# The first token group's product with w3 from split fp16 operands, with a new preparation and order of the weights

## The chip, the cores and the metric

The kernel runs on one core of one Trainium2 chip. The metric is the time of one execution on the device in microseconds (us); below, "the time" is the median of the runs shown. TensorE is PE in the profile, its weight loads are PEld, VectorE is DVE, ScalarE is ACT, GpSimd is POOL, and SP is the engine that issues most of the DMAs.

## The reference

Two layers, each of a local dilated attention (block A) and an MLP mixer (block B), are applied twice to 2048 tokens of 512 features. Everything is float32. Cut to what matters:

```
x = A_x
for layer in (0, 1):
    x = x + A(layernorm(x), wqkv, wo)        # 32 heads of 16; each token sees 8 tokens, 2 apart
    x = x + B(layernorm(x), w1, w2, w3, w4)

def B(x, w1, w2, w3, w4):                    # w3: 512 x 1792, w4: 1792 x 512
    h  = gelu(layernorm(x) @ w1)
    hs = (quarters of h shifted by +1, -1, +2, -2 tokens) @ w2
    x1 = x + hs
    return x1 + gelu(layernorm(x1) @ w3) @ w4
```

## The kernel before, in words

**Tiles and groups.** The 2048 tokens are 4 blocks of 512, and each block is 4 tiles of 128 tokens. With two layers there are 8 steps n = 0 to 7, one per layer and block. In step n the functions are: `p1_quarters`/`p1_stream` (layer norm and the product with wqkv; the results go to DRAM and come back with the neighbours' rows), `p2_unit` (the attention itself, almost all on VectorE: a product `prod<-kv,q`, a reduction into `L`, a softmax, a product `prod<-kv,L`, additions), `p3` (the product with wo, then norm and w1), `p4` (shift, the product with w2, norm), `p5` (w3, gelu, w4). Because w2 needs shifted rows, `p4` and `p5` work on a *group* of tiles that lags by one tile: group 0 has 3 tiles (384 tokens), later groups have 4, the last has 5.

**Split operands.** Most products replace one float32 product by three fp16 products. Each operand is written as hi + lo, two fp16 numbers, and `HLS` (line 50) names the three pairs hi·hi, hi·lo and lo·hi that are summed in PSUM. The weights wqkv, wo, w1, w2 are split on the chip near the start and kept. w3 and w4 are 14 chunks each; they are split by `big_pair` (line 912) and stored in DRAM as `w34_d`. A pair is two chunks of w3 and two of w4: four loads, four squares on ScalarE with a sum (tile `ss_p`), a product with ones and a power that give the scale (`power_of`, line 541), and for each chunk `hi_of` (583), `rest` (590) and a DMA that stores it. `p5` loads them again for each group (`w<-w` in the profile).

**Group 0 is the exception** (`PLAIN = 1`, line 1242). Its normalized tiles are turned by TensorE in float32 (`turn_f32`, line 698) and copied by ScalarE into `nT`. For each chunk, `plain_chunk` (line 1297) loads w3 and w4 once more in float32 straight from the input, forms the w3 product in float32 (four matmuls 128x128 by 128x384, which the profile records as eight), applies gelu, and forms the w4 product in float32 (three matmuls of 512 columns, recorded as six). Later groups turn their tiles by DMA (`turn_dma`, line 675): ScalarE writes the hi half, VectorE or GpSimd the lo half, and SP issues one DMA transpose.

**What sets the order.** Every operation gets a number in the order in which the code creates it. The list `PLACES` (line 56) gives each its place in one global order, written out by hand. `plan` (line 268) walks that order, gives out buffers, and issues each operation on its engine; `InOrder` (line 328) keeps each engine's instructions in that order (all instructions carry line 338 in the profile for this reason). `OTHER` (line 196) lists the operations that take their second alternative, mostly GpSimd in place of VectorE or ScalarE. The durations in the code feed only `plan`'s choice of buffers. Each engine, and SP's queue of DMAs, is therefore a fixed sequence: an instruction that waits holds up all that stand behind it on its engine.

**Buffers that matter here.** `w` (8), `g` (5), `nT` (2), `mm` (4 PSUM banks), `prod` (1) and `kv` (3).

Of the kernel before, what the change touches and what calls it, by code (L numbers as in the profile page):

```python
# [56 lines left out]
15 29 72 33 3 148 0 1 6 5 19 12 8 13 7 21 40 58 20 45 2 4 14 16  # L57
17 9 10 11 24 26 18 22 23 30 31 36 37 39 48 50 28 35 25 27 44 46 42 43
49 53 47 55 54 63 51 62 71 76 201 67 61 110 64 90 73 98 74 109 177 422 132 117
92 119 111 156 112 165 130 169 396 311 275 391 104 137 168 221 202 203 236 237 360 374 252 413  # L60
96 75 204 115 41 52 32 34 56 59 38 57 60 65 77 79 80 91 94 121 86 93 82 95
81 99 85 102 87 103 84 101 83 100 131 114 136 158 159 174 175 176 195 246 285 239 313 322
323 364 384 435 524 462 523 155 186 213 218 267 289 321 575 339 588 488 499 434 437 526 558 551
574 547 578 482 538 589 591 598 603 611 618 620 623 685 694 642 645 693 668 669 670 900 922 823
845 864 912 868 924 932 939 943 952 958 965 987 978 998 1000 953 973 1021 961 972 1053 433 436 408
409 426 431 387 432 438 453 470 472 561 581 604 508 566 567 473 485 573 483 491 634 891 908 870
981 886 942 928 944 982 1008 1013 1020 1034 1035 1046 1027 1030 1044 1070 1087 1088 1085 1110 1121 786 787 781
782 799 801 780 804 808 816 821 826 860 861 862 838 839 847 834 836 925 865 866 927 1023 1048 969
994 977 1005 1007 1052 1054 1068 1076 1082 1111 1123 1144 1083 1089 1092 1086 1107 1108 1131 1148 1175 146 199 153
183 135 219 150 184 232 234 235 244 258 516 637 305 331 543 309 325 358 260 282 452 105 144 253  # L70
97 318 278 506 448 1084 78 70 69 152 68 66 107 127 133 140 141 149 160 166 167 191 192 193
205 208 220 212 216 223 229 280 290 296 128 116 120 126 171 154 198 222 145 164 151 210 211 245
250 257 277 281 283 287 300 304 335 301 308 317 348 349 394 403 170 173 182 181 310 217 243 306
224 242 249 263 279 299 314 329 350 353 359 376 380 388 397 390 400 410 411 412 416 423 273 270
297 298 332 405 371 407 357 366 361 381 392 393 398 399 402 404 415 418 420 442 444 419 441 443
451 458 465 466 106 108 122 123 124 138 147 194 196 230 185 188 190 189 178 179 200 180 88 89
125 129 143 162 163 225 227 238 226 228 233 231 240 264 268 265 241 271 291 319 320 324 328 356
368 373 363 395 445 446 369 379 417 421 157 161 207 274 276 288 292 336 370 378 326 362 377 375
333 334 337 338 450 454 622 477 512 533 560 521 520 705 577 582 593 614 616 621 641 644 662 671
687 688 695 698 701 702 703 704 707 708 753 721 722 725 727 735 736 737 744 748 749 784 592 597  # L80
752 633 658 706 713 610 571 732 666 667 678 686 731 733 734 742 743 755 759 760 761 762 763 764
765 766 771 777 805 767 768 769 770 772 773 774 775 809 810 811 113 142 187 197 209 214 215 261
272 284 247 259 266 262 269 293 295 294 172 206 248 251 254 255 256 302 303 312 307 315 342 347
316 327 346 341 286 365 383 385 386 401 427 430 484 504 428 455 486 487 464 490 517 503 118 134
139 340 343 367 372 389 414 447 382 459 481 460 406 425 480 468 696 692 849 745 747 820 822 783
803 802 829 850 856 888 889 892 899 905 906 909 910 911 915 917 929 940 948 957 1091 1149 1232 963
975 993 1003 1022 1037 1045 1058 1119 1130 1239 872 933 1161 1067 1079 1094 1095 835 966 1170 1112 1113 1127 1128
1136 1137 1141 1151 1152 1177 1179 1180 1181 1182 1183 1186 1187 1197 1199 1210 1225 1198 1207 1208 1209 1212 1214 1215
1233 1234 1237 1238 344 345 429 440 457 463 469 497 519 544 471 505 522 518 545 556 584 576 351 352
474 475 476 479 489 525 546 548 511 535 947 848 554 579 580 632 534 536 537 557 559 583 602 664  # L90
697 710 890 914 945 986 657 718 751 788 461 478 552 553 555 568 572 635 663 665 817 831 951 832
601 612 837 625 1206 1043 1263 1235 1242 1271 1277 1224 1226 1292 1248 1253 1257 1258 1278 1293 1294 1295 1303 1304
1306 1321 1322 1323 1324 1325 1327 1338 1402 1418 1421 1483 1484 1485 1486 1489 1490 1492 1493 1531 1532 1562 1320 1218
1401 1343 1344 1363 1364 1366 1367 1420 1377 1381 1403 1404 1415 1419 1430 1435 1436 1437 1439 1455 1461 1462 1468 1469
1470 1471 1480 1497 1543 1503 1521 1522 1525 1526 1527 1528 1529 1534 1545 1565 456 330 354 439 355 424 449 467
492 493 500 501 502 527 532 496 498 513 514 515 529 530 494 495 507 528 539 540 541 509 510 531
542 549 550 562 605 563 569 570 587 617 590 564 585 586 600 852 565 595 596 599 628 630 594 606
# [1337 lines left out]
```

## Time and profile before

| what | value |
|---|---|
| runs | 1142.68, 1144.0 and 1894.58 us; median 1144.0 us |
| the profiled execution's own time | 1145.03 us |
| its span, first to last instruction | 1143.2 us |
| mean granted TensorE clock | 0.997 |
| busy PE / DVE / ACT / POOL | 98% / 75% / 54% / 37% |
| DMA moved | 206.37 MB, mean 181 GB/s |

The profiled execution's time is 1.8 us longer than its span; the median of the runs is 1.03 us below that time. In a timeline row stand the start, the length, the engine, the line, the operation with out<-in, the count that was merged, and in brackets the idle time before it with what ended it. In a row of stages stand the stretch, its length, and for PE, PEld, DVE, ACT and POOL the busy time with the number of instructions, then the granted clock, the DMA engines' busy share and GB/s. A matmul's recorded length overlaps the next one's, so the cost of a run of matmuls is read from start to start.

### The profile page before, as it was taken

Reading aid. Unit: us, or ns where it says so; the run is one execution under the profiler, and the core shown is the slowest. Engines: PE = TensorE matmul, PEld = TensorE weight load, DVE = VectorE, ACT = ScalarE, POOL = GpSimd, SP = SyncE. Lnnn points to the kernel's source line nnn. Section 1 sums busy time; section 2 is a strip of 40 time slices with the busy share of each in tenths; the row PEclk is TensorE's granted clock in tenths of the full one; section 3 lists DMA queues with packets and bytes.
Section 4 is the critical chain, followed back from the end, with each engine's and each line's share of the span. In section 5 each row is a group of like instructions: output and inputs, shape, how many; then the busy total and the mean of one; then the engine's idle time right before and its main releaser. Section 6 shows DMA issues by size and latency. Waiting matters only on the chain.

```text
span 1143.2 us, 15112 instructions
## 1 busy us (share of the span) xinstructions
PE 1124.1 (98%) x5190; PEld 532.4 (47%) x5190; DVE 862.6 (75%) x919; ACT 618.6 (54%) x1089; POOL 417.9 (37%) x596
## 2 busy tenths in 40 slices
PE   8989999999999999999999999999999999999998
PEld 6544445554444444444444444444444444444554
DVE  4989899997899998988888888378986888323212
ACT  4766785247863565464654565354555554535321
POOL 4342364125652571135534353252324342322000
PEclk9999999999999999999999999999999999999999
DMA  6988989997989669974679756596687865524322
GB/s 175 217 205 215 223 216 259 256 238 182 265 234 222 162 161 211 244 187 121 161 182 230 192 136 166 128 237 177 154 206 166 199 168 158 113 75 112 100 88 79
DMA packets 249165, 206.37 MB, mean 181 GB/s; under 512 B 131032, under 2 KB 192472, under 8 KB 249088
## 3 DMA queue, kind: packets, MB, share of 16 engines
q1 hardware_dynamic: 247472, 203.63, 72.3%
q10 hardware_dynamic: 1616, 1.77, 0.5%
q8 instruction: 41, 0.67, 0.2%
q14 instruction: 36, 0.29, 0.1%
HBM read 132.64 MB, written 37.87 MB: 149 GB/s over the span
## 4 chain that ended last, share of the span: by engine, by line
PE 60%; ACT 2%; DVE 1%; issue 1%; POOL 1%; POOLq 0%; DVEq 0%; ACTq 0%
PE mm L338 42%; PE acc L338 18%; POOL small L338 1%; ACT f L338 1%; DVE L L338 0%; DVE prod L338 0%; ACT junk L338 0%; DVE f L338 0%; ACT L338 0%; ACT g L338 0%; ACT mm L338 0%; POOL f L338 0%; DVE x L338 0%; POOL o L338 0%; DVE h L338 0%
## 5 line engine op out<-in xcount | busy, mean ns | idle before, releaser
L338 PE MATMUL acc<-w,g 128*128 128x512 f16 (+1 forms) x1260 | 307.3, 394 | 0.0
L338 PE MATMUL mm<-nT,w 128*128 128x512 f16 (+1 forms) x1288 | 301.7, 389 | 0.8 <-ACT f L338 0.8
L338 PE MATMUL mm<-wq_hl,xt 128*128 128x512 f16 x1008 | 226.8, 381 | 3.2 <-DMA xt<-f 2.3
L338 ACT ACTIVATE mm<-mm,s_w 128x512 f32<-128x512 f32 (+1 forms) x144 | 89.7, 628 | 195.0 <-PE mm L338 194.7
L338 PEld LDWEIGHTS <-w 128*128 128x128 f16 x1344 | 125.2, 98 | 142.2 <-issue 1.0
L338 PEld LDWEIGHTS <-g 128*128 128x128 f16 x1176 | 114.7, 98 | 137.5
L338 DVE TENSOR_TENSOR prod<-kv,L 128x2048 f32<-128x2048 f32 x64 | 148.7, 2325 | 13.6 <-POOL o L338 12.2
L338 PEld LDWEIGHTS <-xt 128*128 128x128 f16 x1008 | 98.8, 98 | 122.5 <-issue 4.8
L338 DVE TENSOR_REDUCE L<-prod 128x128 f32<-128x2048 f32 x64 | 146.2, 2284 | 1.2
L338 POOL TENSOR_SCALAR small<-small 128x1 f32<-128x1 f32 (+1 forms) x200 | 88.8, 444 | 137.8 <-ACT junk L338 123.8
L338 DVE TENSOR_TENSOR prod<-kv,q 128x2048 f32<-128x2048 f32 x58 | 134.3, 2316 | 3.7 <-DMA q<-q_d 1.9
L338 DVE TENSOR_TENSOR prod<-prod 128x512 f32<-128x512 f32 (+2 forms) x109 | 111.5, 1026 | 2.7
L338 POOL TENSOR_TENSOR g<-f,g 128x512 f16<-128x512 f32 x39 | 54.8, 1409 | 117.8 <-ACT g L338 69.2
L338 DVE SCALAR_TENSOR_TENSOR g<-mm,c_g,g 128x512 f16<-128x512 f32 x56 | 41.5, 745 | 63.7 <-ACT g L338 63.7
L338 PE MATMUL mm<-w_hl,h 128*128 128x512 f16 x384 | 85.7, 379 | 1.1 <-POOL h L338 1.1
L338 PE MATMUL mm<-nT,w_hl 128*128 128x512 f16 x384 | 86.5, 379 | 0.0
L338 POOL TENSOR_TENSOR small<-small,nhalf 128x1 f32<-128x1 f32 (+1 forms) x104 | 72.3, 695 | 8.7
L338 PE MATMUL mm<-wo_hl,oT 128*128 128x512 f16 x336 | 74.3, 379 | 0.0
L338 POOL TENSOR_TENSOR prod<-prod 128x512 f32<-128x512 f32 (+1 forms) x24 | 30.5, 1271 | 105.9 <-DVE prod L338 99.4
L338 ACT ACTIVATE ev<-mm,s_kv 128x512 f32<-128x512 f32 x56 | 38.1, 681 | 54.8 <-PE mm L338 40.0
L338 ACT ACTIVATE g<-mm,c_g 128x512 f16<-128x512 f32 x98 | 66.6, 684 | 1.9
L338 PEld LDWEIGHTS <-oT 128*128 128x128 f16 x426 | 41.5, 98 | 49.0 <-issue 0.6
(188 smaller groups left out, 1217.8 us busy)
## 6 DMA issues: line engine op xcount, KB each, us to landing
w<-w SPq DMA_DIRECT2D x196, 256.0 KB
kv<-kv_d SPq DMA_DIRECT2D x112, 352.0 KB
w<-in_B_w_dram SPq DMA_DIRECT2D x56, 256.0 KB
kv_d<-ev SPq DMA_DIRECT2D x112, 128.0 KB
q_d<-ev SPq DMA_DIRECT2D x28, 256.0 KB
w<-g SPq DMA_DIRECT2D x28, 256.0 KB
q<-q_d SPq DMA_DIRECT2D x28, 256.0 KB
x<-x SPq DMA_DIRECT2D x26, 256.0 KB
```

What stands on the lines that cost most here:

```text
L338: i = f(*a, **k).ins
```

## The change

Group 0's w3 product takes the same three fp16 products as the others, from the split `w34_d`, at a width of 384; its w4 product stays in float32. The w3 loads in float32 of `p5(0)` (14 of 256 KB) become loads of `w34_d`. Group 0's three tiles are turned by DMA. w3 and w4 are split in groups of four chunks (4, 4, 4, 2), all of w3 ahead of all of w4, and the scale `s_w3` is made per group of w3 chunks.

```diff
-BY_DMA = {"p1": 1, "p2": 1, "p3": 1, "p4": 1}
+BY_DMA = {"p1": 1, "p2": 1, "p3": 1, "p4": 0}
...
-    def big_pair(c, key):
+    def big_four(k, j, key):
...
-    iv = [big_pair(c, KW + 0.6 + 0.2 * c) for c in range(NP)]
+    iv = [big_four(k, j, KW + 0.6 + 0.4 * k + 0.1 * j) for k in range(2) for j in range(len(FOURS))]
...
+        if k == 0:
+            def inverse():
+                v = s_w3.t[:, cs[0]:cs[0] + len(cs)]
+                V.tensor_scalar(v, iv4.t, SN, None, ALU.mult)
+                V.reciprocal(v, v)
+            dve(key, 0.3, inverse, [iv4], [(s_w3, j)])
...
-            if n < PLAIN:
-                turn_f32(key + 0.01 * k, nr, dst, [(dst, (k, 0))], lambda dst=dst, k=k: f32v(
-                    dst.t, NC * D).rearrange("p (c t) -> p c t", c=NC)[:, :, P * k:P * (k + 1)])
-            else:
+            if True:
...
-    def plain_chunk(c, key, w3, w4, acc, nT):
+    def plain_down(c, key, ps, w4, acc):
...
-        def up():
-            for k in range(NC):
-                T.matmul(ps.t[:, :P * K], f32v(w3.t, D)[:, P * k:P * (k + 1)],
-                         f32v(nT.t, NC * D)[:, D * k:D * k + P * K], start=(k == 0), stop=(k == NC - 1))
...
                 pe(key, 12 * (wd * 0.000417 + 0.0025), up,
-                   [w3, (nT, [(k, a) for k in range(k0, k1) for a in range(2)])], [ps, (g, "new")])
+                   [w3, (nT, [(k, a) for k in range(k0, k1) for a in range(2)])], [ps, (g, "new")] if g else [ps])
+                if n < PLAIN:
+                    dma(key - 0.0015, lambda w4=w4: f32v(w4.t, D), lambda c=c: w4_d[P * c:P * (c + 1), :],
+                        [], [w4], 1.0, begun)
+                    plain_down(c, key, ps, w4, acc)
+                    continue
```

`plan`'s model of the port that VectorE and GpSimd share, and some durations in the code, change as well; they feed only its choice of buffers. The lists `PLACES` (3291 numbers, then 3302) and `OTHER` (132, then 140) are new throughout. Counted off these lists, with the operations numbered as the code creates them, the order on TensorE around group 0 is:

| TensorE's work, by place | before | after |
|---|---|---|
| last w2 product of group 0 | 631 | 653 |
| wqkv products of block 3 between it and the first w3 product | 635, 657, 664 | 656, 674, 675 |
| turning group 0's three tiles | 647, 653, 661 (TensorE) | 677, 685, 686 (SP, by DMA) |
| first w3 product of group 0 | 674 | 687 |
| first wo product of block 1 | 818 | 842 |
| w3 products and w4 products of group 0 ahead of it | 13 and 10 | 13 and 11 |
| further wqkv products ahead of the first wo product of block 3, and of step 4 | - | 1, and 2 |
| last VectorE operation of block 1's attention | 810 | 835 |
| VectorE and GpSimd operations up to that one | 204 and 63 | 207 and 80 |

Of the two later tiles of group 0, the lo halves are made by GpSimd (places 680 and 681); the first tile's by VectorE (667).

More of the change, by code (lines that the diff above doesn't have):

```diff
@@ L276, in plan @@
             pool[kind].remove((0.0, j))
-    dma_free, port, table, order = 0.0, 0.0, None, []
+    dma_free, port, wide, table, order = 0.0, 0.0, 0.0, None, []
     for o in sorted(ops, key=lambda o: o.key):
@@ L300, in plan @@
                 d += TABLE
-            if e == POOL or cls == "lock":
-                begin = max(begin, port)
+            if e == POOL:
+                if begin < port:
+                    begin = max(begin, port - GRANT)
+                if cls != "tiny":
+                    wide = begin + d - GRANT
+            elif cls == "lock":
+                begin = max(begin, wide)
                 port = begin + d
@@ L307, in plan @@
             free[e] = o.end - TAIL[e]
+            if cls == "tiny":
+                o.end += HELD
         order.append(o)
@@ L1310, in down @@
                          start=(c == 0), stop=(c == NF - 1))
[L1311 removed]
         act(key, 0.15 + 0.115 * K, lambda: A.activation(f32v(g.t, D)[:, :P * K], ps.t[:, :P * K],
[L1313 removed]
+                                                       AF.Gelu_apprx_tanh, scale=s_w3.t[:, c:c + 1]),
+            [ps, (s_w3, c // 4)], [g], cls=GELU)
         pe(key, 0.8585 * K, down, [w4, g], acc)
```

87 lines of the change are left out of this document (40 added, 47 removed), and 288 rows, old and new, of tables (OTHER, PLACES).

## The prediction

> **What bounds the kernel now.** I read the page's busy times first, then a table of stages, then the timeline of each engine around group 0.
>
> ```profile
> span 1143.2 us, 15112 instructions
> PE 1124.1 (98%) x5190; PEld 532.4 (47%) x5190; DVE 862.6 (75%) x919; ACT 618.6 (54%) x1089; POOL 417.9 (37%) x596
> ```
> ```profile
> 60.00:134.00 74.00, 69.64 (x323) 32.94 (x323) 62.82 (x78) 50.38 (x98) 22.61 (x26) 0.98 0.90 218
> 134.00:185.00 51.00, 50.10 (x246) 24.10 (x244) 48.69 (x56) 43.93 (x79) 30.74 (x47) 1.00 0.96 232
> 185.00:273.00 88.00, 88.00 (x272) 44.66 (x271) 82.75 (x75) 34.92 (x63) 26.85 (x32) 1.00 0.97 248
> 273.00:600.00 327.00, 323.15 (x1499) 146.24 (x1498) 288.06 (x305) 193.08 (x325) 149.12 (x184) 1.00 0.79 191
> 600.00:1138.50 538.50, 538.50 (x2620) 248.84 (x2618) 337.11 (x351) 258.57 (x430) 164.25 (x248) 1.00 0.61 152
> ```
>
> TensorE is busy for 1124.1 of 1143.2 us, and after 600 us without a gap, so work taken off it is worth its full length there. But the stages differ: from 60 to 273 us VectorE is busy for 194 of 213 us too. It prepares the attention of block 1, which TensorE needs for its first wo product of that block:
>
> ```profile
> 242.40 2.33 SPq L338 DMA_TRANSPOSE oT<-f  x1
> 247.29 5.34 PE L338 MATMUL mm<-wo_hl,oT 128*128 128x512 f16 x24
> ```
>
> The last transpose of the attention's result is issued by 242.40 + 2.33 = 244.73, and TensorE uses it at 247.29. How long such a transpose takes to land is seen where TensorE did wait for one:
>
> ```profile
> 119.06 1.28 SPq L338 DMA_TRANSPOSE xt<-f  x1
> 122.72 5.35 PE L338 MATMUL mm<-wq_hl,xt 128*128 128x512 f16 x24 [0.65 <-DMA xt<-f]
> 77.13 1.80 SPq L338 DMA_TRANSPOSE xt<-f  x1
> 84.63 7.95 PE L338 MATMUL mm<-wq_hl,xt 128*128 128x512 f16 x36 [1.62 <-DMA xt<-f]
> ```
>
> From the end of the issue that is 122.72 - 120.34 = 2.4 us, and 84.63 - 78.93 = 5.7 us. At 2.4 us the data for 247.29 arrived at about 247.1: TensorE and VectorE meet there with 0.2 us to spare. The same sum for blocks 2 and 3:
>
> ```profile
> 368.44 3.27 SPq L338 DMA_TRANSPOSE oT<-f  x2
> 376.10 10.52 PE L338 MATMUL mm<-wo_hl,oT 128*128 128x512 f16 x48
> 475.14 1.93 SPq L338 DMA_TRANSPOSE oT<-f  x1
> 480.59 10.52 PE L338 MATMUL mm<-wo_hl,oT 128*128 128x512 f16 x48
> ```
>
> 376.10 - 371.71 - 2.4 = 2.0 us, and 480.59 - 477.07 - 2.4 = 1.1 us. So the question is less what TensorE saves than whether VectorE lets it arrive earlier.
>
> **The change part by part.** *The w3 products.*
>
> ```profile
> 182.16 0.60 PE L338 MATMUL mm<-ident,f 128*128 128x128 f32 x4
> 182.60 2.75 PE L338 MATMUL mm<-wq_hl,xt 128*128 128x512 f16 x12
> 185.19 5.32 PE L338 MATMUL mm<-nT,w 128*128 128x384 f32 x16
> 190.35 2.74 PE L338 MATMUL acc<-w,g 128*128 128x512 f32 x6
> 1060.37 1.50 PE L338 MATMUL mm<-xt,w 128*128 128x128 f16 x24
> 1061.71 2.75 PE L338 MATMUL acc<-w,g 128*128 128x512 f16 x12
> ```
>
> From start to start, two float32 w3 products take 190.35 - 185.19 = 5.16 us, 2.58 each. Twelve fp16 matmuls of 512 columns take 185.19 - 182.60 = 2.59, 0.216 each; 24 of 128 columns take 1061.71 - 1060.37 = 1.34, 0.056 each. No row has 384 columns. It lies between, and the straight line gives 0.056 + 2/3 x 0.160 = 0.163, so 1.95 us per product. I take that; the ends are 0.67 and 2.59 us, the last of which would make the step worth nothing. Saved: 14 x 0.63 = 8.8 us.
>
> *The turning by DMA.* Three float32 turns on TensorE go, 182.60 - 182.16 = 0.44 each, 1.3 us. So TensorE does 10.1 us less. In exchange the chain from the last w2 product to the first w3 product grows:
>
> ```profile
> 175.94 2.75 PE L338 MATMUL mm<-wq_hl,xt 128*128 128x512 f16 x12
> 179.66 0.80 ACT L338 ACTIVATE f<-f,small 128x512 f32<-128x512 f32 x1
> 157.08 0.62 ACT L338 ACTIVATE f<-f 128x512 f16<-128x512 f32 x1
> 155.43 0.68 DVE L338 TENSOR_TENSOR f<-f,f 128x512 f16<-128x512 f32 x1
> 161.27 1.16 POOL L338 TENSOR_TENSOR f<-f,f 128x512 f16<-128x512 f32 x1
> ```
>
> The last w2 product ends at 175.94, and the last tile is normalized at 180.46, 4.5 us later. Then come the hi half (0.62), the lo half (0.68 on VectorE, 1.16 on GpSimd), the issue (1.28) and the landing (2.4 to 5.7): 9.5 to 13.3 us in all. After the change three wqkv products (7.8 us) stand in between and nothing else, and each w3 product reads all three tiles, so TensorE waits for 1.7 to 5.5 us. Before, it did not wait. As both late lo halves are made by GpSimd one behind the other, up to 3.5 us more can come on top (the other half's 1.16, and one VectorE product of 2.3 that holds GpSimd up; the rows of that are below), up to 9.0. The DMA engines are 96% busy in this stage, so I take a landing in the middle, and 4 us. A wait has a second price:
>
> ```profile
> 61.93 0.38 PE L338 MATMUL mm<-ss_w,ones 128*128 128x1 f32 x2 [1.90 <-ACT ev L338]
> 62.50 6.91 PE L338 MATMUL mm<-wq_hl,xt 128*128 128x512 f16 x24 [0.19 <-ACT ev L338]
> 62.00:64.00 2.00, 1.81 (x6) 0.79 (x7) 0.00 (x0) 2.00 (x7) 0.00 (x0) 0.57 0.63 168
> ```
>
> After about 2.4 us almost idle the granted clock was 0.57, and 24 matmuls took 6.91 us where the wo products' 24 took 5.34: 1.6 us lost. The waits of 1.62 and 0.65 us above cost nothing of the kind (7.95 us for 36, 5.35 for 24). With it the wait takes 5 to 6 us. The Trainium skill (TensorE: Matmul & The Clock Gate, "What's actually happening") puts this down to a gate that halves the clock after an idle window of about 3.4 us and opens it after as much work; by that figure the loss could be up to an estimated 1.7 us. The trace agrees in size, though here some 2.4 us of idling were enough.
>
> *What the wait costs in the end.* By the places, 13 w3 products and the turns, 9.5 us of savings, lie ahead of block 1's first wo product, but one more w4 product (2.58, as the six records from 190.35) is put ahead of it: 6.9 us less. With the wait TensorE comes there 1 to 2 us earlier. So the wait at the turn costs nothing as long as VectorE isn't earlier by more than that; it is paid out of time that TensorE would spend waiting for the attention. From 6.9 us on it decides.
>
> *VectorE.* Up to the end of block 1's attention it has 204 operations before and 207 after. It loses four lo halves of activations (about 0.7 each, as in the row of 155.43) and one of a weight to GpSimd, and gains one lo half of group 0, four scale steps of w3, a square of wqkv and some small ones; the sum is within 0.5 us of what it was. So by its work alone it is ready at the same time. What can move is its idle time, 213 - 194 = 19 us from 60 to 273.
>
> *The weights.*
>
> ```profile
> 189.53 1.05 SPq L338 DMA_DIRECT2D w<-g  x2
> 149.86 0.63 ACT L338 ACTIVATE junk<-w 128x512 bf16<-128x512 f32 x1
> 157.60 0.71 ACT L338 ACTIVATE g<-w,inv_p 128x512 f16<-128x512 f32 x1
> ```
>
> Three pairs were split ahead of group 0, the last two stores at 189.53: 6 chunks of w3 and 6 of w4. Now it is 14 of w3, two chunks more: for each, a square (0.63) and a hi half (0.71) on ScalarE, 2.7 us in a stage where it is busy for 44 of 51 us. Their cover is TensorE's wqkv products of blocks 1 to 3. The first chunk's store (place 448) is far ahead of its product, so I cost this at nothing; without the cover it is those 2.7 us, ahead of the chain above, and a chunk that is late shows as a wait for `w`. Group 0's w3 loads keep their number and size. w4's split moves behind, and has until group 1.
>
> **The sum.** If VectorE's idle time stays as it is, each block's attention sets a limit: the spare time at its wo product, plus what VectorE has less to do, plus the work that TensorE has less behind that point. Block 1: 0.2 + 0 + (10.1 - 6.9) = 3.4 us. Block 2: 2.0 + at most 2 + 0, since no difference is left behind it: about 4. Block 3: 1.1 + 0.7 (VectorE's operations counted off the lists as for block 1) + 2.6 (one wqkv product more is put ahead) = 4.4. So the gain is at least about 3.4 us if nothing gets worse, and at most 10.1 us unless waits of before vanish too. Between these I take 6, as if VectorE lost some 3 of its 19 idle us: its order is new throughout and some 20 operations more are GpSimd's, which frees it in places. The profiled execution's own time, 1145.0, would go to 1139.0; the median of the runs, 1.0 below it, to **1138 us**.
>
> **The rivals.** *TensorE's saving comes through whole.* VectorE would have to be 7 us earlier by block 1. For it: 11 of its idle us lie between 60 and 134 us. Against it: it has as much work as before. 1144 - 10.1 = 1134 us, or 1129 if half of TensorE's idle time in mid-run (some 9 us of its 19) goes as well.
>
> *Nothing is left.* The turn by DMA takes the long end: a wait of 9.0 us, with the clock 10.6, is 3.7 above the 6.9, which eats the 3.2 us behind. 1144 us. For it: the full DMA engines and the two lo halves on GpSimd. Against it: transposes of later blocks stay near the short end. That the fp16 products don't gain at 384 columns ends here too.
>
> *Slower: GpSimd in VectorE's way.* Up to block 1's attention GpSimd gets 17 operations more (63 to 80).
>
> ```profile
> 163.83 3.00 POOL L338 TENSOR_TENSOR inv_p<-mx,nhalf 128x4 f32<-128x4 f32 x1 [1.36 <-DVE mx L338]
> 163.67 2.28 DVE L338 TENSOR_TENSOR prod<-kv,q 128x2048 f32<-128x2048 f32 x1
> 189.01 1.26 POOL L338 TENSOR_TENSOR x<-x,f 128x512 f32<-128x512 f32 x1
> 189.69 2.73 DVE L338 TENSOR_TENSOR prod<-kv,L 128x2048 f32<-128x2048 f32 x1
> ```
>
> A tiny power takes 3.00 us beside a VectorE product, and a product that started under a GpSimd addition takes 2.73 in place of 2.28. If each added operation holds VectorE up by 0.45 us, that is 7.7 us by block 1, more than the 3.4 us of gain, and the point from which it decides. With some 9 operations more by block 4, 4 us, the time is 1144 - 3.4 + 7.7 + 4 = about 1152 us. Against it: most VectorE products keep 2.29 us, so GpSimd is usually the one that waits. The Trainium skill (SBUF — State Buffer, "SBUF: two separate sides") says that whichever of the two starts first holds the pair for its whole instruction; by that rule an added 1.16 us operation could hold VectorE up fully, an estimated 20 us for 17, and the time would be near 1160. The trace shows such holds, but mostly on GpSimd's side.
>
> **How the numbers follow.** Forecast (1134.5 to 1141): 0.48. Whole saving or more: 0.20. Nothing left (1141 to 1147): 0.17. Slower by GpSimd or another new wait: 0.15. The range of 1129 to 1151 us takes in the rivals' prices and leaves out the ends of the last and second. Two per cent, about what a measurement of this kernel can tell from no change, is 23 us: faster than 1121 would need the whole saving and all of the idle time, 0.02; slower than 1167 would need twice the slow rival's price, 0.03; so 0.95 within.
>
> **What would show it.** Right: records `mm<-nT,w 128x384 f16` x168 with 0.16 us from start to start; 12 float32 turns fewer; a wait of 2 to 6 us for `nT` ahead of the first w3 product, with a granted clock under 1 just behind it; block 1's first wo product at 243 to 247 us; TensorE's busy time lower by about 10 us. Wrong: that wo product behind 248 us or ahead of 241, waits for `w`, or VectorE products lengthened as a group.

## The result, and the profile after

The changed kernel takes 1157.3 us (median of four runs, 1156.15 to 1160.53), the kernel before 1144.2 us in the same session. The ratio is 1.0124, with a 95% interval of 1.0097 to 1.0151: slower by 13 us, where 6 us of gain were forecast. The profiled execution took 1160.5 us, some 3 us above the median, with a mean granted clock of 0.990 where the other three runs had 0.992 to 0.996; up to about that much of its length is its own.

The page of the changed kernel:

```profile
span 1158.7 us, 15203 instructions
PE 1124.7 (97%) x5236; PEld 529.5 (46%) x5236; DVE 892.9 (77%) x930; ACT 611.9 (53%) x1078; POOL 504.8 (44%) x613
```

TensorE's w3 products are shorter, and yet it is busy as long as before (1124.1): 0.7% less of its clock (a mean of 0.990 where before had 0.997) is, by an estimate from these two means, some 8 us of its busy time. Its idle time grew from 19.1 to 34.0 us. VectorE is busy for 30 us more, GpSimd for 87.

The timeline of TensorE in the changed kernel, around group 0:

```profile
181.06 2.75 PE L346 MATMUL mm<-wq_hl,xt 128*128 128x512 f16 x12
184.17 5.35 PE L346 MATMUL mm<-wq_hl,xt 128*128 128x512 f16 x24 [0.36 <-DMA xt<-f]
195.45 8.70 PE L346 MATMUL mm<-nT,w 128*128 128x384 f16 x36 [5.93 <-DMA nT<-f]
203.99 2.74 PE L346 MATMUL acc<-w,g 128*128 128x512 f32 x6
206.57 2.11 PE L346 MATMUL mm<-nT,w 128*128 128x384 f16 x12
208.52 5.31 PE L346 MATMUL acc<-w,g 128*128 128x512 f32 x12
254.63 5.56 PE L346 MATMUL mm<-wo_hl,oT 128*128 128x512 f16 x25
```

A w3 product takes 208.52 - 206.57 = 1.95 us, as forecast. The wait for the turned tiles is 5.93 us, and the three products behind it take 203.99 - 195.45 = 8.54 instead of 5.85 us, so 2.7 us of clock are lost: 8.6 us together. The granted clock was 0.50 from 195.45 to about 201 us and 1.00 behind it, and half of these 5.5 us is the loss. (The expectations below speak of "the wait of 8.7 us"; the wait alone is 5.93.) But group 0's last w2 product had ended at 181.06, where it ended at 175.94 before: 5.1 us of lateness had come in ahead of the wait, and it did not leave. Block 1's first wo product, the place that the prediction watched, comes at 254.63 instead of 247.29. From the first w3 product to there TensorE does not wait once (in the row below its busy time is the whole stretch), so its own account closes: 5.1 us late at the last w2 product, 9.0 us for the waits (0.36 and 5.93) and the clock, 6.9 us less work as forecast, 7.2 us late at the wo product, where 7.3 are measured.

```profile
195.45:254.63 59.18, 59.18 (x236) 29.82 (x237) 55.40 (x49) 20.23 (x36) 14.04 (x11) 0.95 0.93 247
```

The stretches between the first wo products of blocks 1, 2 and 3 (a row: the stretch, its length, busy time and number of instructions for PE, PEld, DVE, ACT, POOL, then the clock, the DMA share and GB/s). Before:

```profile
20.00:247.29 227.29, 222.03 (x892) 113.27 (x891) 206.84 (x220) 140.08 (x283) 80.66 (x102) 0.99 0.91 222
247.29:376.10 128.81, 127.52 (x567) 58.29 (x566) 114.55 (x133) 85.45 (x151) 65.88 (x73) 1.00 0.90 229
376.10:480.59 104.49, 103.80 (x481) 46.91 (x480) 94.20 (x98) 58.99 (x96) 39.04 (x59) 1.00 0.85 190
```

After:

```profile
20.00:254.63 234.63, 221.34 (x948) 111.79 (x947) 215.85 (x227) 143.95 (x290) 127.18 (x143) 0.97 0.85 221
254.63:380.15 125.52, 124.46 (x565) 56.94 (x564) 112.99 (x125) 76.52 (x133) 63.55 (x76) 1.00 0.89 230
380.15:494.79 114.64, 108.70 (x493) 48.21 (x492) 102.85 (x101) 64.08 (x106) 51.25 (x64) 0.99 0.72 165
```

Up to block 1's wo product the stretch is 7.3 us longer. VectorE's busy time grew by 9.0 us, and its idle time even fell, from 20.5 to 18.8 us. It was not kept waiting: its own work took longer. Nearly all of that, 8.9 us, lies ahead of group 0's last w2 product, and so belongs to the 5.1 us. Before, then after:

```profile
20.00:175.94 155.94, 150.68 (x666) 75.76 (x665) 137.30 (x162) 115.89 (x241) 61.72 (x85) 0.99 0.87 210
```
```profile
20.00:181.06 161.06, 154.06 (x677) 78.59 (x676) 146.19 (x164) 115.27 (x241) 101.98 (x122) 0.98 0.83 217
```

VectorE's groups of operations up to the wo product show which got longer. Before:

```profile
L338 DVE TENSOR_REDUCE L<-prod 128x128 f32<-128x2048 f32 x18 | 41.1, 2283 | 0.2
L338 DVE SCALAR_TENSOR_TENSOR wq_hl<-h,inv_q,wq_hl 128x1152 f16<-128x1152 f32 x4 | 5.4, 1412 | 0.0
L338 DVE SCALAR_TENSOR_TENSOR g<-w,inv_p,g 128x512 f16<-128x512 f32 x7 | 5.0, 733 | 0.0
L338 DVE TENSOR_TENSOR f<-f,f 128x512 f16<-128x512 f32 x7 | 4.8, 686 | 4.2 <-ACT f L338 4.2
L338 DVE SCALAR_TENSOR_TENSOR h<-mm,c_h,h 128x512 f16<-128x512 f32 x4 | 2.9, 744 | 0.0
```

After:

```profile
L346 DVE TENSOR_REDUCE L<-prod 128x128 f32<-128x2048 f32 x18 | 41.0, 2276 | 0.2
L346 DVE SCALAR_TENSOR_TENSOR g<-w,inv_p,g 128x512 f16<-128x512 f32 x8 | 8.6, 1070 | 1.2 <-ACT g L346 1.2
L346 DVE SCALAR_TENSOR_TENSOR wq_hl<-h,inv_q,wq_hl 128x1152 f16<-128x1152 f32 x4 | 7.4, 1856 | 1.2 <-ACT wq_hl L346 1.2
L346 DVE TENSOR_TENSOR f<-f,f 128x512 f16<-128x512 f32 x4 | 4.1, 1020 | 0.0
L346 DVE SCALAR_TENSOR_TENSOR h<-mm,c_h,h 128x512 f16<-128x512 f32 x4 | 2.9, 744 | 0.0
```

These three groups, each with two operands in SBUF, got longer by a third to a half (733 to 1070 ns, 1412 to 1856, 686 to 1020). Reductions, with one operand, and operations that read PSUM (`mm`) kept their length to 1%. Summed over the forms that both kernels have, against each form's mean of before, VectorE loses some 11 us to longer operations up to block 1's wo product and some 17 up to block 3's; the rest of its work is one to two us less. GpSimd's operations got longer as well. Two of its groups up to the wo product, before and then after:

```profile
L338 POOL TENSOR_TENSOR g<-w,g 128x512 f16<-128x512 f32 x5 | 5.8, 1160 | 0.4
L338 POOL TENSOR_TENSOR f<-f,f 128x512 f16<-128x512 f32 x5 | 5.8, 1158 | 12.6 <-ACT f L338 12.6
```
```profile
L346 POOL TENSOR_TENSOR g<-w,g 128x512 f16<-128x512 f32 x8 | 11.2, 1396 | 0.7
L346 POOL TENSOR_TENSOR f<-f,f 128x512 f16<-128x512 f32 x9 | 12.7, 1410 | 18.4 <-ACT f L346 18.4
```

How the operations of both get longer, in the timeline of VectorE and then of GpSimd in the changed kernel:

```profile
188.96 2.28 DVE L346 TENSOR_TENSOR prod<-kv,q 128x2048 f32<-128x2048 f32 x1
191.16 1.64 DVE L346 SCALAR_TENSOR_TENSOR g<-w,inv_p,g 128x512 f16<-128x512 f32 x1
192.73 2.27 DVE L346 TENSOR_REDUCE L<-prod 128x128 f32<-128x2048 f32 x1
```
```profile
189.03 3.23 POOL L346 TENSOR_TENSOR f<-prod,f 128x512 f16<-128x512 f32 x1 [0.21 <-ACT f L346]
```

GpSimd's subtraction starts just behind VectorE's product and takes 3.23 us instead of 1.16. Read with the product's end at about 191.2, it stands still until then. Then it runs, to 192.26, and now VectorE's next operation with two SBUF operands stands still: 1.64 us instead of 0.74. The reduction behind it is untouched.

### The profile page after: what moved, and what is told of

Its sections match the earlier page's. It is cut to its first block, busy times and chain, and to the rows that moved or that the text cites. A ratio compares the mean times of both kernels' runs of the same rounds, so it can differ in the third digit from the quotient of the medians.

```text
span 1158.7 us, 15203 instructions
## 1 busy us (share of the span) xinstructions
PE 1124.7 (97%) x5236; PEld 529.5 (46%) x5236; DVE 892.9 (77%) x930; ACT 611.9 (53%) x1078; POOL 504.8 (44%) x613
## 4 chain that ended last, share of the span: by engine, by line
PE 67%; DVE 11%; POOL 9%; issue 4%; DMA 4%; ACT 4%; SPq 1%; POOLq 0%; DVEq 0%; ACTq 0%
PE mm L346 45%; PE acc L346 22%; POOL small L346 6%; DVE prod L346 5%; DVE L L346 3%; SPq L346 1%; DMA w<-in_A_x_dram 1%; POOL f L346 1%; ACT f L346 1%; ACT junk L346 1%; DMA w<-w 1%; DMA kv<-kv_d 1%; DVE mx L346 1%; DVE f L346 1%; DMA nT<-f 1%
## 5 line engine op out<-in xcount | busy, mean ns | idle before, releaser
L346 PE MATMUL mm<-nT,w 128*128 128x512 f16 (+1 forms) x1344 | 296.4, 375 | 6.9 <-DMA nT<-f 6.1
L346 PE MATMUL mm<-wq_hl,xt 128*128 128x512 f16 x1008 | 229.2, 383 | 5.5 <-DMA xt<-prod 3.0
L346 PEld LDWEIGHTS <-w 128*128 128x128 f16 x1512 | 142.3, 98 | 164.7 <-issue 15.6
L346 POOL TENSOR_SCALAR small<-small 128x1 f32<-128x1 f32 (+1 forms) x200 | 126.0, 630 | 173.5 <-ACT junk L346 158.9
L346 DVE TENSOR_TENSOR prod<-kv,L 128x2048 f32<-128x2048 f32 x64 | 151.8, 2372 | 7.4 <-POOL o L346 4.0
L346 DVE TENSOR_TENSOR prod<-prod 128x1024 f32<-128x1024 f32 (+2 forms) x118 | 126.0, 1069 | 4.2 <-ACT prod L346 1.2
L346 POOL TENSOR_TENSOR small<-small,nhalf 128x1 f32<-128x1 f32 (+1 forms) x104 | 84.7, 814 | 8.7
L346 PEld LDWEIGHTS <-w_hl 128*128 128x128 f16 x384 | 37.4, 98 | 48.4 <-issue 4.6
```

What stands on the lines that cost most here:

```text
L346: i = f(*a, **k).ins
```

## The experiments

Every ratio is against the kernel before on the same chip. "wo(1)" is the start of block 1's first wo product: 247.29 before, 254.63 after. Each is read from one trace. Three runs below have the same order up to there, and it comes at 250.08, 247.13 and 246.72 in them, so a difference of some 3 us in it says little; VectorE's busy time up to there is steadier (207.96, 207.75 and 207.35 us in the same three).

### Order and product, each alone

`old_order_fp16`: before's lists, the product in fp16, turned by TensorE.

```diff
-            k, i = m // 2, 2 * c + m % 2
+            k, i = divmod(GLOB[c][m], NF)
...
-                turn_f32(key + 0.01 * k, nr, dst, [(dst, (k, 0))], lambda dst=dst, k=k: f32v(
+                turn_pe(key + 0.01 * k, nr, dst, [k], lambda cols=cols: cols(0), lambda cols=cols: cols(1), [nr])
...
+                dma(key - 0.003, lambda w3=w3: w3.t, lambda c=c: w34_d[c % 12][:, 0].rearrange("p a f -> p (a f)"),
+                    [(w34, (c % 12, 0))], [w3], 1.0)
```

> The order of before, with every number of its list kept, but group 0's w3 product is the three fp16 products: the first three groups of four that are split hold w3's chunks 0 to 11, and group 0's tiles are turned by TensorE and split into hi and lo from PSUM (three more VectorE operations of about 0.7 us). Chunks 12 and 13 of group 0 read the halves of chunks 0 and 1, in size and time the same, so part of the output is another. Theory A (the loss comes from the new order: waits and slow clock, not from the product): about 8.8 us of TensorE work go and at most 2 to 3 us of waits for the lo halves come back: 1136 to 1141 us. Rival B (group 0's fp16 chain itself costs the time, in any order): a wait of 6 us or more ahead of the first w3 product with a slow clock behind it, 1146 us or more. Rival C (VectorE's attention of block 1 sets the limit, so that the work that goes is waited for): 1143 to 1146.

Measured: 1149.2 us, 1.0033 (1.0015 to 1.0052), wo(1) at 249.57.

`new_order_f32`: after, with before's product and turn.

```diff
-                   [w3, (nT, [(k, a) for k in range(k0, k1) for a in range(2)])], [ps, (g, "new")] if g else [ps])
+                   [w3, (nT, [(k, a) for k in range(k0, k1) for a in range(2 if n else 1)])],
...
+                    if n < PLAIN:
+                        for k in range(NC):
+                            T.matmul(ps.t[:, :wd], f32v(w3.t, D)[:, P * k:P * (k + 1)],
```

> The order, the GpSimd list and the split of w3 and w4 of after, but group 0's w3 product is the float32 product of before, from w3 loaded in float32, with its tiles turned by TensorE in float32. Theory A (the new order loses by itself): TensorE has 10.1 us more work than after, and loses the wait of 8.7 us for the turned tiles and its clock loss: 1155 to 1162 us. Rival B (group 0's fp16 chain costs the time): the 15 us of loss were its own, so the time falls back to that of before: 1143 to 1148.

Measured: 1159.3 us, 1.0122 (1.0101 to 1.0144).

`new_order_turn_pe`: after, with group 0's tiles turned by TensorE.

```diff
-                if n >= BY_DMA["p4"]:
+                if n >= 1:
```

> The kernel after, with group 0's three tiles turned by TensorE and split from PSUM (hi on ScalarE, lo on VectorE) in place of the turn by DMA; all else as after. If the turn by DMA costs the wait of 8.7 us and 2.7 us of clock at the first w3 product (rival B), most of it goes: 1146 to 1150 us. By theory A the tiles were late before they were turned (the last w2 product ended 5 us later than in before), and VectorE stands behind: 1152 to 1158.

Measured: 1158.6 us, 1.0128 (1.0097 to 1.0160).

`old_order_fp16_dma`: the first of these four, turned by DMA (`turn_dma` for every n), with the three lo halves on GpSimd.

```diff
-            if n >= 1:
+            if n >= 0:
                 turn_dma(key + 0.01 * k, nr, dst, [k], lambda dst=dst, k=k: (
```

> As the first run (order of before, group 0's w3 product in fp16, chunks 12 and 13 with the halves of chunks 0 and 1), but group 0's tiles are turned by DMA and their three lo halves made by GpSimd, so that VectorE has nothing more to do than before. If VectorE's three added operations made the loss of 5 us: 1143 to 1146, although TensorE waits 6 to 11 us for the turned tiles. If that wait costs its length: 1150 or more.

Measured: 1156.5 us, 1.0114 (1.0092 to 1.0136), wo(1) at 254.58. VectorE was not spared: 211.78 us busy up to there, against 206.84 before. Together:

| group 0's w3 product | order before | order after |
|---|---|---|
| float32 | 1144.2 | 1159.3 |
| fp16, turned by TensorE | 1149.2 | 1158.6 |
| fp16, turned by DMA | 1156.5 | 1157.3 |

In the new order neither the product nor the turn makes a difference that these runs can tell (ratios 1.0122, 1.0128 and 1.0124). The order, with its list of GpSimd operations and its split by fours, costs 14 to 15 us by itself, and the fp16 product, with 10 us less TensorE work, gives back 2 at most. wo(1) is at 254.63 after, and in the runs with the float32 product and with the turn by TensorE, in that order:

```profile
255.09 10.52 PE L346 MATMUL mm<-wo_hl,oT 128*128 128x512 f16 x48
```
```profile
254.77 10.52 PE L346 MATMUL mm<-wo_hl,oT 128*128 128x512 f16 x48
```

Three kernels with different TensorE work and different waits arrive within 0.5 us of each other. That alone does not show which engine sets the time. With the float32 product TensorE works without a wait from its first w3 product (190.30) to wo(1), and the last transpose of the attention's result is issued by 250.38: with the prediction's 2.4 us of landing the data were there 2.3 us early, and TensorE's own work decides. After, the same sum gives 0.6 us to spare, and with the turn by TensorE 0.4: there the two engines arrive together, as before (0.2). By this reading less work on TensorE could have brought at most some 2 us at wo(1) in the new order. In the old order, too, the fp16 chain lost instead of gaining: VectorE has three more operations of 0.7 us and eight small ones, and is busy for 4.1 us more up to wo(1) (210.90 against 206.84), and TensorE waits for `nT` and then for `g`. Turned by DMA (the last row) it waits far longer than I had allowed for:

```profile
187.53 5.82 PE L338 MATMUL mm<-nT,w 128*128 128x384 f16 x24 [3.88 <-DVE nT L338]
236.20 4.24 PE L338 MATMUL acc<-w,g 128*128 128x512 f32 x6 [4.71 <-ACT g L338]
```
```profile
195.69 6.63 PE L338 MATMUL mm<-nT,w 128*128 128x384 f16 x24 [13.38 <-DMA nT<-prod]
```

### Less work on TensorE alone

`before_less_tensor`: the kernel before, one of four w3 matmuls left out in group 0.

```diff
-            for k in range(NC):
+            for k in range(NC - 1):
...
```

> The kernel before, in which each of group 0's 14 w3 products leaves out the last of its four float32 matmuls (a quarter of the sum is missing): TensorE has 14 x 0.645 = 9.0 us less to do, almost what the change takes off it, and nothing else is touched. The prediction's limits (block 1's attention is ready at the old time, and what lies behind it comes through): a gain of about 3 us, 1140 to 1142 us. Rival (TensorE sets the time, the saving comes through whole): 1135. Rival (VectorE sets it everywhere, or the shorter products only move the waits): 1143 to 1146.

Measured: 1143.8 us, 0.9997 (0.9983 to 1.0012), wo(1) at 247.45. The 9 us are lost to the last one. Most of them are one wait; TensorE's and then ScalarE's timeline of this run:

```profile
232.91 5.45 PE L338 MATMUL acc<-w,g 128*128 128x512 f32 x6 [5.55 <-ACT g L338]
```
```profile
230.01 0.72 ACT L338 ACTIVATE prod<-o,c_o 128x512 f16<-128x512 f32 x1 [11.15 <-DVE o L338]
232.00 1.23 ACT L338 ACTIVATE g<-mm 128x384 f32<-128x384 f32 x3
```

The row of w4 products takes 5.28 us from start to start instead of 2.58, too: the granted clock behind the wait was 0.50. Three gelus stand on ScalarE behind the hi half of an attention tile, and that waits 11 us for VectorE's `o`. VectorE's attention reaches TensorE not only at the wo product, but ahead of it through ScalarE's queue. VectorE itself was busy for 209.75 us up to wo(1) in this trace, 2.9 more than before with the same operations; how much of the 9 us went there the run does not tell.

### More and less work on GpSimd

`before_more_gpsimd`: 21 idle subtractions added to the kernel before.

```diff
+    scr = Buf("f32")
...
+        G.tensor_sub(scr.t, scr.t, scr.t)
+    for q in range(21):
+        gp(0.0, 1.2, lambda q=q: extra(q == 0), [], [scr])
```

> The kernel before with 21 more GpSimd operations, each one subtraction of 128x512 float32 on a tile that nobody else uses, spread evenly by place from 240 to 812 (some 60 us to block 1's wo product). After has about that many more wide GpSimd operations up to there. Theory D (GpSimd holds up VectorE's operations that read two operands from SBUF, some 0.43 us for each wide GpSimd operation): VectorE's busy time up to block 1's wo product grows by about 9 us, that product comes at 253 to 257 instead of 247, the time is 1150 to 1156. Rival E (GpSimd only waits for VectorE and not the other way; the new order is late for its sequence): VectorE's busy time unchanged, the time within 3 us of before.

Measured: 1152.3 us, 1.0071 (1.0047 to 1.0095); wo(1) at 253.56. VectorE, with the same 220 operations, is busy for 217.88 instead of 206.84 us, 0.53 us for each subtraction on average (wo(1) is 6.3 us later; the rest of the 11.0 comes out of VectorE's idle time):

```profile
20.00:253.56 233.56, 221.94 (x895) 112.89 (x893) 217.88 (x220) 140.27 (x284) 120.49 (x124) 1.00 0.88 215
```

`after_less_gpsimd`: the kernel after, 22 operations taken off GpSimd.

```diff
+OTHER.update({k: 2 for k in (138, 185, 188, 207, 210, 232, 235, 250, 509, 569, 629, 665, 839, 1012, 1022)})
...
+        by_act = (ACT, 0.186 + n * 0.00103, lambda: A.activation(lo(), src(), AF.Copy, scale=scale), None)
-        op(key, alts + [(POOL, 0.24 + n * 0.00335, by_pool, None)] * last, r, w)
+        op(key, alts + [(POOL, 0.24 + n * 0.00335, by_pool, None), by_act] * last, r, w)
```

> The kernel after, in whose order 22 operations that GpSimd has up to block 1's attention go to ScalarE: four hi halves, three normalizations, and 15 lo halves, for which ScalarE writes a scaled copy in place of the remainder (the lo halves are then not the reference's). ScalarE gets some 16 us more, VectorE not one operation more or less. Theory D: VectorE's busy time up to block 1's wo product falls by about 9 us, that product comes at 246 to 250 instead of 254.6, the time is 1146 to 1152 (the rest of the loss comes from later blocks). Rival E (the sequence itself is late): VectorE stays as it is or is later, 1156 or more.

Measured: 1151.3 us, 1.0068 (1.0048 to 1.0089). VectorE's 9.0 us are gone but for 1.1, wo(1) comes 4.5 us earlier (7.5 and 7.9 in the two other runs with this order up to there), and 6 of the 13 us are back. Group 0's last w2 product ends at 176.66, and at 175.23 and 173.43 in those two: the 5.1 us of lateness there are gone. The work was not taken away but given to ScalarE, which is busy for 12 us more (155.74 against 143.95):

```profile
20.00:250.08 230.08, 218.97 (x951) 111.62 (x950) 207.96 (x227) 155.74 (x311) 81.97 (x112) 0.98 0.88 226
```

`before_less_gpsimd` and `before_less_both`: eight of before's GpSimd lo halves cut to 16 columns, without and with the shorter w3 products. The lines are those of the five halves of weights; the three of activations are cut in the same way.

```diff
+OTHER.update({k: 2 for k in (178, 181, 187, 226, 235, 639, 675, 813)})
...
+            G.tensor_scalar(src()[:, :16], src()[:, :16], scale, 1.0, ALU.mult, ALU.mult)
+            G.tensor_sub(lo()[:, :16], src()[:, :16], hi()[:, :16])
```

`before_less_gpsimd`:

> The kernel before, in which eight lo halves that GpSimd makes ahead of block 1's wo product (three of activations, five of weights with two operations each) are made for 16 of 512 columns only; the rest of these halves is left out. 13 wide GpSimd operations become small ones, and no other engine has more or less to do. Theory D (about 0.43 us of VectorE for each wide GpSimd operation): VectorE's busy time up to block 1's wo product falls by 5 to 6 us, that product comes 2 to 5 us earlier, the time is 1138 to 1142. Rival F (TensorE, 98% busy, sets the time of before, and GpSimd only hurts where VectorE is already late): 1143 to 1145.

`before_less_both`:

> The run before this one with the shorter w3 products of the run with less TensorE work (9.0 us less, one of four matmuls left out). If the saved TensorE work counts only as far as VectorE's attention is ready earlier (theory D with the prediction's limits): 2 to 5 us below the run before this one, 1134 to 1139. If the saving is lost in any case: as the run before this one.

Measured: 1142.1 us, 0.9980 (0.9966 to 0.9995), and 1142.2 us, 0.9990 (0.9976 to 1.0004). VectorE's busy time did not fall:

```profile
20.00:243.70 223.70, 220.65 (x890) 113.07 (x889) 207.09 (x220) 139.83 (x283) 77.42 (x102) 0.99 0.92 225
```

So my price per operation was wrong for these: where before has its GpSimd operations, they cost VectorE nothing (and by the rows above they take 1.16 us there themselves, where after they take 1.4). It is the place beside VectorE's operations that costs, not the number. wo(1) did come 3.6 us earlier in the first of the two traces (243.70), as forecast, but out of VectorE's idle time, and that is about what single traces differ by; the time is 0.2% less. And as VectorE was not relieved, the shorter w3 products gained nothing here either (wo(1) at 245.21, with a wait of 5.17 us for `g` at 231).

`before_rest_on_vector`: before's eight two-step lo halves of w3 and w4 back on VectorE, by eight entries less (178 to 304) in `OTHER`, whose first line becomes:

```diff
- 27 37 100 101 104 107 116 178 181 187 226 235 256 277 304 361 366 396 421 422 425 465 483 566
+ 27 37 100 101 104 107 116 361 366 396 421 422 425 465 483 566 569 572 639 675 710 711 728 770
```

> The kernel before, in which the eight lo halves of w3 and w4 that GpSimd makes in two operations are made by VectorE in one of about 0.74 us (five of them ahead of block 1's wo product); the result is the same. Theory D: two wide GpSimd operations cost VectorE about 0.9 us, more than the 0.74 us of doing it itself, so VectorE's busy time falls by about 1 us and the time is 1141.5 to 1144. If GpSimd's operations cost VectorE less than that: VectorE has up to 4 us more to do up to block 1's wo product, 1145 to 1149.

Measured: 1147.4 us, 1.0029 (1.0014 to 1.0045). VectorE is busy for 211.55 us up to wo(1), 4.7 more, and takes that from its idle time, as wo(1) stays at 247.36. Same lesson: there GpSimd did this work for nothing.

`before_new_model`: before's lists with after's planner model.

```diff
-LAT, LAT_PE, LAT_SP, LAT_DMA, LEAD, TABLE, COLD = 0.06, 0.4, 0.15, 1.5, 0.85, 1.3, 1.0
+LAT, LAT_PE, LAT_SP, LAT_DMA, LEAD, TABLE, COLD = 0.06, 0.35, 0.15, 1.5, 0.85, 1.3, 1.0
+GRANT, HELD = 0.14, 0.6
```

> The kernel before with its own order and its own list of GpSimd operations, but with the planner's model and the durations of after (the port's GRANT and HELD, the wait of TensorE, the tiny class). They feed only the choice of buffers. Theory D: no difference, 1142 to 1146. Rival G (part of the loss comes from other buffers): 1148 or more.

Measured: 1143.8 us, 1.0003 (0.9989 to 1.0017). In before's order the choice of buffers has no share. wo(1) is at 245.83, with VectorE busy for 208.17 us.

### The second half of the loss

Between the wo products of blocks 2 and 3 the changed kernel takes 114.64 us instead of 104.49. One wqkv product more (2.6 us) stands there; the rest is waits, where before had one of 0.69 us, and the slow clock behind them:

```profile
418.95 9.62 PE L346 MATMUL mm<-wq_hl,xt 128*128 128x512 f16 x36 [2.14 <-DVE h L346]
440.16 2.12 PE L346 MATMUL mm<-w_hl,h 128*128 128x512 f16 x9 [0.59 <-POOL h L346]
458.19 5.35 PE L346 MATMUL mm<-wq_hl,xt 128*128 128x512 f16 x24 [2.96 <-DMA xt<-prod]
```

Five runs went for it. `new_then_old` has after's lists up to place 1230 and before's behind; `less_gpsimd_then_old` the same with the 22 operations off GpSimd; `after_less_gpsimd_far` takes GpSimd's work off up to place 1600; the last two, `less_gpsimd_turn_pe` and `less_turn_pe_then_old`, have group 0 turned by TensorE as well (the `if n >= 1:` above). The old order behind place 1230 is a new list `PLACES`, of which one line, and `OTHER` of before from there on; the "far" run adds one edit for the residual additions:

```diff
- 966 1000 1001 1002 1144 1145 1197 1019 1031 1032 1042 1046 1090 1102 1105 1169 1177 1253 1040 1048 994 1120 1121 1140
+ 966 1000 1001 1002 1144 1145 1197 1019 1031 1032 1042 1046 1090 1102 1105 1169 1177 1261 1040 1048 994 1120 1121 1140
```
```diff
+            fc = slice(0, 16 if 842 <= PLACES[len(op.ops)] < 1600 else D)
-            op(key + 0.3, [(POOL, 1.25, lambda src=src, x1=x1: G.tensor_add(src(), src(), x1.t), None),
+            op(key + 0.3, [(POOL, 1.25, lambda src=src, x1=x1, fc=fc: G.tensor_add(
+                src()[:, fc], src()[:, fc], x1.t[:, fc]), None),
```

`new_then_old`:

> The kernel after, with its own order up to place 1230 (just ahead of block 2's wo product) and from there the order and the GpSimd list of before. Theory A in its second half (some 7.5 of the 25 us that after loses come from the new order between the wo products of blocks 2 and 3): 1147 to 1152 us. Rival (VectorE is late from the first 250 us on and hands this on, whatever the order behind): 1155 to 1160.

Measured: 1155.2 us, 1.0090 (1.0067 to 1.0112).

`less_gpsimd_then_old`:

> As the run of after with 22 GpSimd operations made by ScalarE up to block 1's attention, and from place 1230 on the order and the GpSimd list of before. If the new order behind makes the second loss: the stretch between the wo products of blocks 2 and 3 takes 105 to 108 us, the time is 1145 to 1148. If not, or if the state that the first part hands on makes it: 1149 to 1153, as in the run with the old order behind the unrelieved first part, which gained 2 us.

Measured: 1151.0 us, 1.0057 (1.0036 to 1.0078).

`after_less_gpsimd_far`:

> As the run of after with 22 GpSimd operations made by ScalarE, and in the places from 842 to 1600 (block 1's wo product to behind block 3's) the same again: 14 lo halves are written by ScalarE as scaled copies, five operations of GpSimd go back to ScalarE, ten lo halves of gelu's result are copied by ScalarE, and the additions of x that GpSimd has there are made for 16 of 512 columns. VectorE's operations stay what they are. If GpSimd makes the second loss as it made the first (theory D): VectorE's busy time between the wo products of blocks 2 and 3 falls from 102.9 to 99 us or less, that stretch from 115.5 to 109 to 112 us, the time is 1145 to 1148. If the order makes it: 1150 to 1153.

Measured: 1151.6 us, 1.0068 (1.0044 to 1.0093). The stretch between the wo products of blocks 2 and 3 takes 111.12 us and VectorE's busy time in it falls to 98.78, both as by the first forecast, yet the time did not follow. Up to block 3's wo product VectorE is busy for 411.7 us, 4 less than before, but idle for 9 more, and ScalarE has 26 us more to do: the test exchanged one load for another.

`less_gpsimd_turn_pe`:

> As the run of after with 22 GpSimd operations made by ScalarE, but group 0's three tiles are turned by TensorE (hi on ScalarE, lo on VectorE from PSUM, two VectorE operations more). If the turn by DMA decides once VectorE is relieved: block 1's wo product comes at 244 to 247 us instead of 250, the time is 1146 to 1149. If VectorE or something else still decides there: 249 to 251 us, and 1150 to 1153.

Measured: 1155.0 us, 1.0091 (1.0068 to 1.0114), wo(1) at 248.24.

`less_turn_pe_then_old`:

> The run before this one with the order and the GpSimd list of before from place 1230 on. If the new order behind has a share of its own, now that the first part is as early as in before: 1 to 4 us below the run before this one. If the loss between the wo products of blocks 2 and 3 comes from what the first part hands on (its VectorE work that stands behind instead of ahead of block 2's wo product): the same as the run before this one.

Measured: 1151.3 us, 1.0062 (1.0044 to 1.0080), wo(1) at 251.05. All of these side by side, each from its trace:

| run | wo(1) | VectorE busy, 20 us to wo(1) | first wo product of block 2 to that of block 3 |
|---|---|---|---|
| before | 247.29 | 206.84 | 104.49 |
| `before_new_model` | 245.83 | 208.17 | 105.27 |
| after | 254.63 | 215.85 | 114.64 |
| `new_then_old` | 254.59 | 215.63 | 110.67 |
| `after_less_gpsimd` | 250.08 | 207.96 | 115.49 |
| `less_gpsimd_then_old` | 247.13 | 207.75 | 111.98 |
| `after_less_gpsimd_far` | 246.72 | 207.35 | 111.12 |
| `less_gpsimd_turn_pe` | 248.24 | 206.79 | 115.62 |
| `less_turn_pe_then_old` | 251.05 | 206.87 | 109.29 |

With the old order behind place 1230 the time falls by 2.1 us (1157.3 to 1155.2), by 3.7 (1155.0 to 1151.3) and by 0.3 (1151.3 to 1151.0); the intervals of each pair overlap, so the times alone do not show a share of that order. The traces do: the stretch takes 113.3 to 115.6 us in the five traces with the new order throughout and GpSimd's work behind place 842 unchanged, and 109.3 to 112.0 in the three with the old order behind place 1230. (Two of the five are the runs with the float32 product, 114.75, and with the turn by TensorE, 113.33.) That is some 4 of the 10 us, and 1 to 2 of these return behind it: from there to the end of the span four of the five take 660.2 to 661.5 us, the three 662.4 to 662.6. What stays in the stretch with the old order there, some 5 us, no run explains. The turn by DMA is not what is left: without it the time did not fall (1155.0 against 1151.3, and 1151.3 against 1151.0). Some 7 us of the 13, those that stay when VectorE is relieved up to block 1, are placed by the traces between the wo products of blocks 2 and 3, but no run took them away, and most of their cause stays open. No kernel here that does all of the work beat the one before.

## Why the prediction was wrong

*What bounds the kernel.* Right, and stronger than I put it. In before's order 9 us less TensorE work gave nothing (0.9997), most of it lost to a wait that leads back to VectorE's attention. After, TensorE and the attention again meet at wo(1) within 0.6 us, only later.

*The w3 products.* Right: 1.95 us each, 168 records of 384 columns. But the 8.8 us bought nothing, as just said.

*The turning by DMA.* Mis-sized: the wait of 5.93 us lies a little above 1.7 to 5.5, inside the 9.0; the clock loss was 2.7 us, not 1.6, and above the 1.7 that the prediction estimated as the most, as the clock stayed at 0.50 for 5.5 us; 8.6 together instead of 5 to 6. The chain was longer in its first links: the last tile was normalized at 188.29, 7.2 us behind the last w2 product instead of 4.5, and its lo half took 3.23 us, while the transposes, issued by 193.51, were used 1.9 us later. So the 6.9 us of saved work did not cover it, and by TensorE's account above it would have come to wo(1) 2 us late even without the 5.1 us from ahead. Whether the turn alone then costs anything is not seen in the new order (1157.3 by DMA, 1158.6 by TensorE, where TensorE waits for other things). In the old order the turn, with three lo halves moved to GpSimd, made a wait of 13.4 us and cost some 7 us (1156.5 against 1149.2).

*VectorE: the step that failed.* "By its work alone it is ready at the same time. What can move is its idle time." The idle time hardly moved, 20.5 to 18.8 us. The work moved: almost the same operations took 9.0 us longer, because more of GpSimd's operations fell beside VectorE's. I counted operations at their durations of before and took these for fixed. Taking GpSimd's work off in that order brought VectorE back to 207.4 to 208.0 us and wo(1) to between 246.7 and 250.1, and adding idle work to before's order did the reverse. From there the sum goes wrong: a gain of "at least 3.4 us" at block 1 became a loss of 7.3, some 5 from VectorE and some 2 from the turn. The limit at block 3, a gain of 4.4, became a loss of 14.2, and half of that is only placed, not explained.

*The rival "slower: GpSimd in VectorE's way".* Up to block 1 this is what happened, at 0.15. Its price there, 7.7 us, stands against a VectorE that is 9.0 us longer and a wo(1) that is 7.3 us later, of which 2 are the turn's; that the two figures are so near is in part luck, as eight lo halves in other places cost nothing. Its 4 us for the blocks behind stand against 7 more by block 3 (480.59 to 494.79). I argued against it that "most VectorE products keep 2.29 us". They do, on average: the mean of `prod<-kv,q` went from 2281 to 2303 ns. What gets longer is the short operation that comes next, while GpSimd, having waited for the product, takes its turn. The Trainium skill (SBUF — State Buffer, "SBUF: two separate sides") says that VectorE's operations with two SBUF inputs and GpSimd's that read SBUF exclude each other for a whole instruction. The trace agrees, in the pair at 189 us and in the groups: two SBUF operands longer, reductions and PSUM readers not. By that rule I had put 20 us as the most for 17 operations; it was 11 for 23 more GpSimd instructions (143 to 166, counted from the start of the span).

*The weights, the planner's model.* Right: no wait for `w` ahead of the first w3 products, and the model alone changes nothing in before's order.

*What would show it.* "That wo product behind 248 us" and "VectorE products lengthened as a group" were named as signs of being wrong; the first came in full, the second for the short operations only.

## What to carry to other kernels

Before costing saved work on the busiest engine, ask which queue delivers what it needs: here 9 us less on an engine that is 98% busy were worth nothing. And an operation moved to GpSimd is not free: 21 of them spread evenly cost VectorE 0.53 us each on average, while eight lo halves in their places of before cost it nothing. VectorE's operations with two SBUF operands got longer, reductions and PSUM readers did not, so a new order must be judged by what runs beside what, not by counts of operations.

## What the runs showed of the hardware

The exclusion works by turns in the pair at 189 us: GpSimd waits out a 2.28 us product, then runs and holds up the next VectorE operation, so 0.74 us became 1.64. A small operation with one SBUF operand can be longer too: VectorE's cut of `inv_p` to int32, 4 columns, went from 160 to 514 ns on average, with up to 1114 ns for one that started beside a GpSimd subtraction:

```profile
L338 DVE TENSOR_SCALAR inv_p<-inv_p 128x4 int32<-128x4 int32 x4 | 0.6, 160 | 0.0
```
```profile
L346 DVE TENSOR_SCALAR inv_p<-inv_p 128x4 int32<-128x4 int32 x4 | 2.1, 514 | 1.1 <-POOL inv_p L346 1.1
```
